# Attention scores in 32 by 32 tiles of TensorE in place of 32 by 128, on one core

## The chip, the core and the metric

The kernel runs on 1 core of a Trainium2 chip. The metric is device time in microseconds (us) for one execution. The core has five engines that run their own instruction streams and meet at semaphores: TensorE (PE in the profile, with its weight loads shown apart as PEld), ScalarE (ACT), VectorE (DVE), GpSimd (POOL) and SyncE (SP, which issues DMAs).

## The reference

The inputs are x (2048 rows of 512), wq (512x512), wk and wv (512x16), wo (512x512), w1 (512x1792) and w2 (1792x512), all bf16. There are 32 query heads of 16 dimensions and a single key/value head that all of them share.

```python
xn = layernorm(x)
q = (xn @ wq) in 32 heads of 16;  k = xn @ wk;  v = xn @ wv
p = softmax(q @ k.T * 16 ** -0.5)
s = (p @ v, heads side by side) @ wo
g = silu(silu(xn @ w1) @ w2)
out = x + s * g
```

The change touches only how the scores q @ k.T are computed.

## The kernel before

**Stages.** The 2048 queries are cut into 4 chunks of 512, the 2048 keys into 16 tiles of 128. Eight groups of four heads each make up a chunk, so there are 32 groups. A block is one head of a group, one key tile and one chunk of queries: 128 keys by 512 queries of scores, one bank of PSUM. After the scores, a block goes through an exponential, and then into the product with the values, which also sums the exponentials (half of the 32 columns of the value operand hold ones, so that the divisor comes out of the same product).

**Exponentials on two engines.** Two blocks of one key tile go to psA[0] or psA[1] (1024 columns each, used in turn), and ScalarE turns them into bf16 weights in one ACTIVATE of 128x1024 (`exp_A`, L655). Other blocks go to psD (two banks, "D" and "D1") or psF, one bank each, and VectorE turns them into a 16-bit integer whose bits are a rough bf16 exponential (`exp_D`, L693); GpSimd adds two shifted copies (`shift`, L718), and the three versions, weighted, are summed in the value product.

**TensorE's shapes.** The 128 by 128 array is used in three tilings:
- row tiles, 32 rows by 128 columns, at `tile_position=(32 * i, 0)`: the scores. The four heads of a group lie in the four row groups of qT and kT, 32 partitions each (16 used), so row tiles i of several blocks can run at the same time, each into a bank of its own. `score` (L616) makes one block's product, `burst` (L629) strings together the products of one call.
- column tiles, 128 rows by 32 columns, at `tile_position=(0, 32 * i)`: the value products (`emit_PV`, L736, recorded at L778, four heads into the four 32-partition quarters of psO), and all dense products for q, the two feed-forward layers and the output projection (`columns`, L399, recorded at L402). Some scores for VectorE are made in this shape too, from a copy of q with the other heads zeroed (`col_fill`, L1349).
- the whole array: transposes, k, v and warm-up products, mostly in the first 30 us.

The last group's first key tiles are done in two halves of 256 queries (`run_half`, L662, product at L671), in row tiles.

**The order.** The program is planned while it is built: the class `Sched` holds each engine's queue, works out the waits from what each operation reads and writes, and keeps a small model of the engines' times. The main loop at L1412 fills the time up to the next score burst with column products, then calls `score_run` (L1271), which issues two blocks for ScalarE (`fill_A`, L646) and, in the same row tiling, blocks for VectorE in the rows that are left (`fill_D`, L1365). In the plan, a burst for ScalarE may start once ScalarE has finished the exponential before last (`release`, L1205), and should start early enough for ScalarE's next (`needed`, L1208). Per ScalarE exponential there is usually one burst of three blocks and two quartets of column products.

The plan charges a row burst by the rows it names and not by the products that are issued in it, so the order of the operations comes from the call below, whatever the closures `made` contain:

```python
return op("pe", f, reads=sorted({k for _, rd in made for k in rd}, key=str), writes=writes,
          cost=("row", [blk[1] for blk, _ in items], NQ))
```

Only the last product of a burst raises the semaphore that ScalarE or VectorE waits for.

Of the kernel before, what the change touches and what calls it, by code (L numbers as in the profile page):

```python
# [13 lines left out]
P = 128  # L14
# [199 lines left out]
def bass_recurrent_scan__grouped_kv_mqa__dense_activation_silu__prompt_kernel(  # L214
# [69 lines left out]
        P=(0.25, 3.0, 0.65, 10, 1.2, 2.0, 0, 12, 0.2, 3, 3, 0.0, 0.35, 0.43, 0, 0.33, 0, 1, 9, 9),  # L284
# [12 lines left out]
        c=(0.2, 3.0, 0.7, 10, 1.6, 2.0, 0, 12, 0.2, 3, 3, 0.0, 9, 0.43, 0, 0.33, 0, 0, 0.6, 9),  # L297
# [3 lines left out]
    with ExitStack() as es:  # L301
        def sb(name, shape, dt=BF16):
            return es.enter_context(nc.sbuf_tensor(name, shape, dt))
# [12 lines left out]
        kT_sb = [sb("kTa_sb", [P, S]), sb("kTb_sb", [P, S])]  # L316
        vaug_sb = sb("vaug_sb", [P, 1 + NPH, NKT, 32])
        qT_sb = sb("qT_sb", [P, 2, NDC, NQ])
# [297 lines left out]
        def score(blk, ap):  # L616
            (gi, kt), i = blk
            c, g = gi // NG, gi % NG
            if ("q", c, g // 2) not in tok:
                raise ValueError(f"no q for {c}, {g}")  # L620
            rd = [("qT", c % 2, g // 2), "qTb", ("kT", 1, kt // 2, i) if g % 2 else ("kT", 0, kt // 2 if kt else "first")]

            def f(e):
                return e.matmul(ap, lhsT=kT_sb[g % 2][32 * i:32 * i + 32, kt * P:(kt + 1) * P],  # L624
                                rhs=qT_sb[32 * i:32 * i + 32, c % 2, g // 2, :],
                                start=True, stop=True, tile_position=(32 * i, 0))
            return f, rd

        def burst(items, writes):  # L629
# [871 lines left out]
        c = NC - 1  # L1501
# [92 lines left out]
```

## Time and profile before

| what | before |
|---|---|
| median of 2 runs | 661.67 us (661.33 to 662.02) |
| the profiled execution | 661.39 us |
| its span, first to last instruction | 659.6 us |
| TensorE products, weight loads | 8199, 8201 |
| score products in row tiles into psA (L624) | 684 + 632, 385 ns each as recorded |
| score products in row tiles into psD (L624) | 325 + 287, 385 ns |
| score products in row tiles into psF (L624) | 34 + 30, 385 ns |
| exponentials on ScalarE (L655) | 662, 630.5 us busy |
| exponentials on VectorE (L693) | 437.2 us busy in psD's two largest groups |
| granted TensorE clock, mean | 0.999 |

The time recorded for one product is longer than the time that the next one has to wait, since products are pipelined and run side by side in different tiles; the distance between starts says more. Two neighbouring exponentials on ScalarE overlap in the same way: 1221 ns is recorded for one, and they start 0.90 us apart when scores are there. A "releaser" is the event that ended an engine's idle time, and the chain of waits follows such events back from the last instruction.

### The profile page before, as it was taken

What the parts mean: (1) busy time and instruction counts of PE and PEld (TensorE: products, weight loads), DVE (VectorE), ACT (ScalarE), POOL (GpSimd) and SP (SyncE); (2) the same over time, 40 slices, a digit from 0 to 9 for tenths busy, and PEclk for the clock granted to TensorE, in tenths of its full rate; (3) what the DMA queues carried; (4) which work ended last, traced back from release to release, by engine and by line L of the source; (5) the groups of instructions that cost most, each with busy time, mean ns of one, the idle gap of its engine ahead of it and who ended that gap; (6) DMA issues with size and microseconds to landing.
All of it is one profiled execution on the core that took longest, in us unless ns stands there. A gap on an engine that the chain in (4) does not pass through costs nothing.

```text
span 659.6 us, 18816 instructions
## 1 busy us (share of the span) xinstructions
PE 649.5 (98%) x8199; PEld 185.3 (28%) x8201; DVE 596.3 (90%) x1023; ACT 652.0 (99%) x754; POOL 384.2 (58%) x388
## 2 busy tenths in 40 slices
PE   9999999999999999999999999999999999999996
PEld 4422222222222222222222222222222222222221
DVE  7999889989889989999989889999989898898995
ACT  8999999999999999999999999999999999999997
POOL 4265665557656647566665656565665565664562
PEclk9999999999999999999999999999999999999999
DMA  5450000000000000000000000010000000000110
GB/s 171 151 164 1 2 8 5 10 2 4 3 2 9 18 26 18 24 3 2 10 1 10 2 3 2 8 33 26 26 3 5 1 10 14 2 2 2 33 34 33
DMA packets 15394, 14.61 MB, mean 22 GB/s; under 512 B 3536, under 2 KB 14800, under 8 KB 15312
## 3 DMA queue, kind: packets, MB, share of 16 engines
q1 hardware_dynamic: 14752, 12.89, 6.5%
q8 instruction: 64, 1.05, 0.7%
q10 hardware_dynamic: 560, 0.52, 0.2%
q14 instruction: 18, 0.15, 0.1%
HBM read 8.95 MB, written 2.10 MB: 17 GB/s over the span
## 4 chain that ended last, share of the span: by engine, by line
ACT 83%; PE 16%; DVE 1%; issue 0%
ACT pa_sb L655 78%; PE psO L778 6%; ACT t_sb L1094 5%; PE psA L624 5%; PE psF L402 3%; PE psF L409 1%; PE psA L671 0%; DVE wq_sb L1527 0%; DVE otr_sb L888 0%; DVE xn_sb L894 0%; PE psD L624 0%; PE psD L478 0%; DVE wq_sb L1522 0%; PE psO L493 0%; DVE onb_sb L890 0%
## 5 line engine op out<-in xcount | busy, mean ns | idle before, releaser
L655 ACT ACTIVATE pa_sb<-psA 128x1024 bf16<-128x1024 f32 x662 | 630.5, 1221 | 0.6 <-PE psA L624 0.6
L718 POOL INT64_ADD ph_sb<-ph_sb x290 | 299.9, 1047 | 197.9 <-DVE ph_sb L693 197.7
L693 DVE TENSOR_SCALAR ph_sb<-psD 128x512 int16<-128x512 f32 (+1 forms) x520 | 348.0, 689 | 34.0 <-PE psD L624 29.2
L778 PE MATMUL psO<-ph_sb,vaug_sb 128*32 128x512 bf16 x1740 | 214.5, 383 | 0.0
L778 PE MATMUL psO<-pa_sb,vaug_sb 128*32 128x512 bf16 (+1 forms) x1332 | 201.3, 382 | 0.6 <-DVE onb_sb L890 0.6
L624 PE MATMUL psA<-qT_sb,kTa_sb 32*128 32x512 bf16 x684 | 132.8, 385 | 2.2 <-ACT pa_sb L655 0.9
L624 PE MATMUL psA<-qT_sb,kTb_sb 32*128 32x512 bf16 x632 | 122.5, 385 | 1.2 <-ACT pa_sb L655 0.5
L624 PE MATMUL psD<-qT_sb,kTb_sb 32*128 32x512 bf16 x325 | 114.3, 385 | 0.0
L718 POOL INT64_ADD x_sb<-x_sb x72 | 74.2, 1043 | 45.6 <-DVE x_sb L693 45.6
L624 PE MATMUL psD<-qT_sb,kTa_sb 32*128 32x512 bf16 x287 | 100.1, 385 | 0.0
L693 DVE TENSOR_SCALAR x_sb<-psD 128x512 int16<-128x512 f32 x132 | 89.2, 684 | 11.4 <-PE psD L624 9.2
L778 PE MATMUL psO<-x_sb,vaug_sb 128*32 128x512 bf16 x432 | 77.6, 383 | 0.0
L624 PEld LDWEIGHTS psA<-qT_sb,kTa_sb 32*128 32x128 bf16 x684 | 32.3, 91 | 142.7 <-ACT pa_sb L655 129.2
L402 PE MATMUL psF<-xnT_sb,w_sb 128*32 128x512 bf16 x896 | 69.8, 384 | 0.0
L402 PE MATMUL psF<-w_sb,u_sb 128*32 128x512 bf16 x896 | 69.5, 384 | 0.0
L624 PEld LDWEIGHTS psA<-qT_sb,kTb_sb 32*128 32x128 bf16 x632 | 29.8, 91 | 135.2 <-ACT pa_sb L655 122.5
L778 PEld LDWEIGHTS psO<-ph_sb,vaug_sb 128*32 128x32 bf16 x1740 | 53.3, 95 | 46.8 <-issue 29.9
L778 PEld LDWEIGHTS psO<-pa_sb,vaug_sb 128*32 128x32 bf16 x1332 | 49.0, 95 | 39.7 <-issue 29.4
L1094 ACT ACTIVATE t_sb<-psF 128x512 bf16<-128x512 f32 x72 | 57.9, 805 | 0.0
L1126 DVE SCALAR_TENSOR_TENSOR u_sb<-t_sb,psF 128x512 bf16<-128x512 bf16 x56 | 38.1, 680 | 4.7 <-ACT t_sb L1094 4.3
L693 DVE TENSOR_SCALAR ph_sb<-psF 128x512 int16<-128x512 f32 x52 | 35.4, 681 | 0.0
L624 PEld LDWEIGHTS psD<-qT_sb,kTb_sb 32*128 32x128 bf16 x325 | 27.6, 91 | 1.8 <-DVE ph_sb L693 1.3
(133 smaller groups left out, 366.7 us busy)
## 6 DMA issues: line engine op xcount, KB each, us to landing
w_sb<-in_B_w_dram SPq DMA_DIRECT2D x2, 1792.0 KB, 7.7
x_sb<-in_A_x_dram SPq DMA_DIRECT2D x18, 128.0 KB, 2.2
qm_sb<-qT_sb SPq DMA_DIRECT2D x64, 32.0 KB, 1.8
out_dram<-ob_sb SPq DMA_DIRECT2D x14, 128.0 KB, 1.7
x_sb<-in_A_x_dram SPq DMA_DIRECT2D x3, 512.0 KB, 6.4
wop_sb<-in_A_wo_dram SPq DMA_DIRECT2D x1, 512.0 KB, 4.4
wq_sb<-in_A_wq_dram SPq DMA_DIRECT2D x1, 384.0 KB, 5.8
x_sb<-in_A_x_dram ACTq DMA_DIRECT2D x2, 128.0 KB, 2.9
```

What stands on the lines that cost most here:

```text
L402: r = e.matmul(bank[32 * i:32 * i + 32, :], lhsT=lhsT[:, 32 * i:32 * i + 32], rhs=rhs, start=start, stop=stop, tile_position=(0, 32 * i), ...
L409: r = e.matmul(bank, lhsT=zero_sb[:, 0:P], rhs=zero_sb[:, :], start=True, stop=True)
L624: return e.matmul(ap, lhsT=kT_sb[g % 2][32 * i:32 * i + 32, kt * P:(kt + 1) * P], rhs=qT_sb[32 * i:32 * i + 32, c % 2, g // 2, :], start=T ...
L655: d = op("a", lambda e: e.activation(pa_sb[:, sl, :], psA[k][:, :], ACT.Exp, scale=ESCALE), reads=["A%d" % k], writes=[("pa", sl)], cost=2 ...
L693: d = op("v", lambda e: e.tensor_scalar(ph_ap(0, sl, 512 * pos, 512 * pos + m), src, float(PH_ONE + PH_BIAS), 0.0, op0=ALU.add, op1=ALU.ma ...
L718: d = op("gp", lambda e, j=j: e.int64_add(ph_ap(j, sl, 0, 4 * NQ).bitcast(I64), ph_ap(0, sl, 0, 4 * NQ).bitcast(I64), PH_SHIFT[j] * 0x0001 ...
L778: r = e.matmul(psO[32 * i:32 * i + 32, cs], lhsT=vaug_sb[:, p["v"], p["kt"], :], rhs=p["ap"], start=s0, stop=s1, tile_position=(0, 32 * i) ...
L1094: op("a", lambda e: e.activation(t_sb[:, n % 2, :], bank_ap(b), ACT.Tanh, scale=0.5 if jb[0] == "h" else 0.25), reads=[b], writes=[("t", n ...
L1126: op("v", lambda e: e.scalar_tensor_tensor(out=dst, in0=t_sb[:, n % 2, :], scalar=1.0, in1=src, op0=ALU.add, op1=ALU.mult), reads=tk["read ...
```

## The change

In `score`, the closure that issued one product of 32 rows and 128 columns issues four of 32 rows and 32 columns. Each takes 32 of the key tile's 128 keys as its weights and writes the 32 partitions of the bank that belong to those keys. The four read the same 512 queries. They stand one behind the other in the burst, at tile positions (32i, 0), (32i, 32), (32i, 64) and (32i, 96).

```diff
             def f(e):
-                return e.matmul(ap, lhsT=kT_sb[g % 2][32 * i:32 * i + 32, kt * P:(kt + 1) * P],
-                                rhs=qT_sb[32 * i:32 * i + 32, c % 2, g // 2, :],
-                                start=True, stop=True, tile_position=(32 * i, 0))
+                for j in range(4):
+                    r = e.matmul(ap[32 * j:32 * j + 32, :], lhsT=kT_sb[g % 2][32 * i:32 * i + 32, kt * P + 32 * j:kt * P + 32 * j + 32],
+                                 rhs=qT_sb[32 * i:32 * i + 32, c % 2, g // 2, :],
+                                 start=True, stop=True, tile_position=(32 * i, 32 * j), skip_group_check=True)
+                return r
             return f, rd
```

Everything else stays as it is: `run_half` keeps its row tiles, the column products keep theirs, and the queues of all engines hold the same operations in the same order, with 7968 products in place of 1992 in the changed lines.

## The prediction

> **What bounds the kernel now.** I read the page first (busy shares, then the chain that ended last), then the timeline of TensorE, of its weight loads and of ScalarE around 300 us, then the start times of the single records, then the waits.
>
> ```profile
> PE 649.5 (98%) x8199; PEld 185.3 (28%) x8201; DVE 596.3 (90%) x1023; ACT 652.0 (99%) x754; POOL 384.2 (58%) x388
> ...
> ACT 83%; PE 16%; DVE 1%; issue 0%
> ```
>
> Two engines are full. The chain runs through ScalarE for 83%, nearly all of it the exponentials of L655, and through TensorE for most of the rest. So ScalarE leads, and TensorE steps in wherever it is late.
>
> ```profile
> 300.32 0.39 PE L624 MATMUL psA<-qT_sb,kTa_sb 32*128 32x512 bf16 x2
> 300.33 0.39 PE L624 MATMUL psD<-qT_sb,kTa_sb 32*128 32x512 bf16 x1
> 300.64 0.62 PE L402 MATMUL psF<-xnT_sb,w_sb 128*32 128x512 bf16 x8
> 301.19 0.39 PE L624 MATMUL psA<-qT_sb,kTa_sb 32*128 32x512 bf16 x2
> 301.20 0.39 PE L624 MATMUL psD<-qT_sb,kTa_sb 32*128 32x512 bf16 x1
> 301.51 0.83 PE L778 MATMUL psO<-ph_sb,vaug_sb 128*32 128x512 bf16 x12
> ```
>
> Here the reader sees one beat: a score burst in row tiles (two products for ScalarE, one for VectorE), a change of tiling, products in column tiles, a change back. From 300.32 to 301.19 is 0.87 us. The records to the nanosecond: the burst's three products start at 300.321, .325 and .328; the first column product at 300.642; its three companions 3 to 4 ns apart; the second four 0.217 us after the last of the first four; the next burst 0.311 us after the last column product. A stream of 512 columns takes 0.213 us (products of 512 columns step by 0.216 us, those of 256, L493, by 0.109, so 256 columns are 0.107), which leaves about 0.10 us for each change of tiling. Counted so over the trace, it is 0.102 us from row to column tiles (633 times) and 0.098 us back (634 times, medians).
>
> ScalarE's exponentials start 0.903 us apart when nothing holds them; with the 72 tanh (0.476 us each) the floor of its stretch is 662 x 0.903 + 72 x 0.4765 = 632 us, and the starts exceed the floor by 9.3 us in sum, at 197 places where the scores came late. TensorE waits in its turn. Counting starts beyond the usual change or step, I find 9.7 us in 205 changes into a score burst, 9.4 us in 103 places within a burst (VectorE's bank not yet free), and 3 us elsewhere: about 22 us. TensorE needs 660 - 22 = 637 us, ScalarE 660 - 9 = 650 us; their mutual waits make the rest.
>
> ```profile
> PEld psA L624 <- ACT pa_sb L655: 251.7, 584, 0.8
> ```
>
> This wait looks like much free time and is not. 251.7 us over 584 is 0.43 us each, and in the timeline above 0.42 us of such a gap is the column products still streaming (0.3 us after the last load) and the 0.1 us change. What is truly free is the 9.7 us above.
>
> **The change, part by part.** It replaces each of 684 + 632 products into psA and 325 + 287 + 34 + 30 into psD and psF, 1992 in all, by four: 5976 more products and as many more loads. The changed program has 7968 of them in the same places and order; no engine's sequence or wait is otherwise different. The half bursts at the end (L671) and the masked scores in column tiles stay.
>
> *The extra tiles.* A burst of three blocks becomes twelve tiles of the array, all different, so their streams can overlap and only their starts are staggered. The nearest row for that is the first quartet after a change into column tiles, where four loads and four products alternate: 3.34 ns per product (mean of 636). Two products in row tiles are 3.4 ns apart (1258 times). I take 3.35 ns: nine more tiles make the usual burst 30 ns longer, and 5976 x 3.35 ns = 20.0 us in all. This lies on TensorE's own path.
>
> The Trainium skill, "TensorE: Matmul & The Clock Gate", section "Measured speedup vs the span model", gives about 4 ns per tile, also for sixteen tiles of 32 by 32. By it the sum would be 23.9 us (an estimate from that page).
>
> *The bounds of one more tile.* Below: nothing, if starts in different row and column groups coincide; no row shows two starts at once, so no gain. Above: the products of L519 (128x16), each with a load of the whole array, start 25 ns apart, which would make 5976 x 25 = 149 us. Loads of 32 columns are nearer to the column quartet (95 ns each there against 91 ns in row tiles, and hidden in both), so I keep 3.35.
>
> *The supply of instructions.* A beat now needs 20 pairs of load and product in 0.9 us, 45 ns a pair, against 11. The densest long stretch is 40 products in 2.2 us, 55 ns each, so the rate is not shown outright. But at 169.75 us TensorE's queue stops in a semaphore instruction for 51 ns; the first load follows at 169.826, and four pairs have all started by 169.867, 65 ns after the stop: 16 ns a pair. Queued instructions need not be that fast, and the drain of 0.1 us before each burst covers the rest: nothing. Fetching them adds 11952 to 18816 instructions; the page has 64 instruction packets at 0.7% of 16 engines' span, 1.2 us each. Some 41 more cost nothing while the DMA engines stand at 0 tenths, and 47 us if each were waited for.
>
> *What is late next.* The scores for ScalarE come 20 ns later in a burst (six more starts) and those for VectorE 30 ns later. Half of the exponentials have less than 0.08 us to spare, so this reaches ScalarE in most beats once TensorE has no rest left. VectorE at 90% has 63 us of gaps and mostly runs behind its banks (it waited for psD only 143 times, 38.5 us), so it takes the delay without becoming the bound.
>
> *The sum.* A beat with two quartets needs 0.869 us of TensorE and now 0.899, against 0.903 of ScalarE: just enough. Beats with three quartets already exceed it and are paid for by rests elsewhere. Of the 20.0 us, what TensorE now waits at changes into a burst, 9.7 us, is taken up, because those rests exist only where it was early; the 9.4 us within bursts are banks that VectorE frees, which I leave as they are. Net +10.3 us. On the profiled execution (661.4 us, its span of 659.6 us and 1.8 us around it; the median of the two runs shown is 661.67): 671.7, say 672 us. Ends of this term: all 22 us of rest taken up, -2 us, which ScalarE's floor turns into about 0 (661); none taken up, +20 us (681).
>
> **Rivals.**
>
> *A: the changes of tiling become cheaper,* since column products and the new scores share 32-column tiles. There are 633 + 634 changes; 16 ns less on each pays for the 20 us, and at half price (0.05 us, 63 us saved) ScalarE alone would bound: 661.4 - 9.3 = 652 us. Against it: counted in the same way, changes of rows or of columns alone are no cheaper (whole array to row tiles 0.098 us, to column tiles 0.094, row tiles to whole array 0.104). That is -1.4%, not a clear gain. Chance 7%.
>
> *B: the change doesn't cost what it says, the delay vanishes in TensorE's rests* or the starts coincide: 659 to 664 us. For it: TensorE's 637 + 20 = 657 us is still less than the span. Against: the rests lie in short pieces next to a full ScalarE. Chance 8%.
>
> *C: more per tile or more waiting,* 5 to 10 ns a pair because loads no longer hide in a burst of twelve, or some instruction packets waited for: 5976 x 7 = 42 us, less 10 of rest, 693 us; 680 to 715 for the span of these. It decides from 4.5 ns per pair upward. Chance 12%.
>
> *D: the four loads of one row of tiles wait for that row's running products.* Then the four streams of a row follow one another: 3 x 0.217 us more in 650 bursts, 423 us, about 1085 us. The column quartets speak against it: there all four tiles share the same 128 rows, and the second load starts 4 ns after the first product. A milder form is 31 ns for each exposed load (the delay from a load at 33.285 us to its product at 33.317): 185 us, about 845. Chance 4%.
>
> The rule behind D is in the Trainium skill, "TensorE: Matmul & The Clock Gate", section "The mechanism": a load overlaps running products only when its row group differs. By that rule D would happen; the trace differs at the column quartets, and no run here shows row and column groups combined.
>
> **How the numbers follow.** The forecast case has 69%, from about 665 to 681 us, likeliest 672. About 2% is what a measurement of this kernel tells from no change: 648.4 and 674.9 us. A third of the forecast case lies above 674.9 (rests less usable than I take), 22%; with C and D slower comes to 38%. Same: 47% of the forecast, A and B, 61%, less 1% for a faster case, as ScalarE's work leaves at most 652 us unless its beat itself shortened. The range leaves out A, part of B, and the upper half of C with D: 663 to 690 us.
>
> **What would show it.** In the profile after: single products of a burst 3 to 4 ns apart, bursts ending 30 ns later (right), or 7 ns and more, or starts 0.217 us apart within a row (C, D). Changes of tiling still 0.10 us; about 0.05 is A. The chain's TensorE share should rise well above 16%, ScalarE should start to show idle time before L655, and rests before bursts should shrink from 9.7 us towards 0. If ScalarE still leads with 83%, B was right. The forecast is wrong if a burst's stagger is other than 3.35 ns per tile, or if VectorE's banks turn out to be the next wait.

## The result and the profile after

The changed kernel takes 668.57 us (median of 2 runs, 668.28 to 668.85) against 661.67 us: 6.9 us more, a ratio of 1.0104 with a 95% interval of 1.0061 to 1.0148. The profiled execution took 668.85 us with a span of 667.0 us, 7.4 us longer than the span before. The forecast was 672 us, in a range of 663 to 690, with a difference within 2% as the likeliest outcome. The times and ratios below are of runs with a granted clock of 0.986 or more; one run of the second experiment with tiny products, at 0.978 and 714.65 us, is left out of them.

The page after, its lines of engines and of the chain that ended last (share of the span, by engine):

```profile
PE 658.5 (99%) x14175; PEld 202.3 (30%) x14177; DVE 599.0 (90%) x1023; ACT 657.4 (99%) x754; POOL 384.2 (58%) x388
...
PE 75%; ACT 21%; DVE 2%; DMA 0%; issue 0%; SPq 0%
```

The busy shares hardly tell that anything happened: both engines were full and still are. The chain does. Before, 83% of it was ScalarE's; now 75% is TensorE's. ScalarE's row shows little more idle time (0.6 us before, 2.6 us now), but the time recorded for one exponential fell from 1221 to 1056 ns: a start that comes late stands less long behind the exponential before it.

```profile
L655 ACT ACTIVATE pa_sb<-psA 128x1024 bf16<-128x1024 f32 x662 | 630.5, 1221 | 0.6 <-PE psA L624 0.6
L657 ACT ACTIVATE pa_sb<-psA 128x1024 bf16<-128x1024 f32 x662 | 623.7, 1056 | 2.6 <-PE psD L625 1.2
```

(The first line is from the page before, the second from the page after.)

The timeline of TensorE (start us, recorded us, line, what, how many) shows one beat of the changed kernel:

```profile
300.37 0.39 PE L402 MATMUL psF<-xnT_sb,wq_sb 128*32 128x512 bf16 x4
300.69 0.41 PE L625 MATMUL psA<-qT_sb,kTa_sb 32*32 32x512 bf16 x8
300.72 0.40 PE L625 MATMUL psD<-qT_sb,kTa_sb 32*32 32x512 bf16 x4
301.04 0.62 PE L402 MATMUL psF<-xnT_sb,wq_sb 128*32 128x512 bf16 x8
301.59 0.41 PE L625 MATMUL psA<-qT_sb,kTa_sb 32*32 32x512 bf16 x8
301.62 0.40 PE L625 MATMUL psD<-qT_sb,kTa_sb 32*32 32x512 bf16 x4
```

The twelve products run side by side: those into psA take 0.41 us together in place of 0.39, and the blocks for VectorE start 0.03 us after those for ScalarE. By the single records, the twelve starts lie between 300.692 and 300.728, 3.3 ns apart, and the column products follow 0.314 us after the last one, as before. The beat is 0.90 us long, it was 0.87.

The waits of TensorE's loads ahead of a burst for ScalarE (us in total, times, longest) stand in three rows, which go by what is taken to have ended the wait: an exponential, a tanh, or nothing that the profile shows. Before, the rows beside the line shown in the prediction were

```profile
PEld psA L624 <- ACT t_sb L1094: 16.5, 39, 0.4
PEld psA L624 <- issue: 7.9, 22, 0.5
```

and now the three are

```profile
PEld psA L625 <- ACT pa_sb L657: 224.9, 537, 0.7
PEld psA L625 <- ACT t_sb L1096: 25.0, 59, 0.4
PEld psA L625 <- issue: 15.4, 43, 0.4
```

47 waits fewer are put down to an exponential, and 41 more to the other two: most of them only changed rows. In sum it is 276.1 us in 645 waits before and 265.3 us in 639 after, 10.8 us less. What is left, 0.42 us each, is little but the column products still streaming and the change of tiling.

**TensorE's ledger.** What a start-to-start count of the records gives, in three sums: starts within score bursts (from the first product of a burst to its last), changes from a burst to column products, and changes back (both beyond the 0.213 us of the last stream, so rests are in them).

| us | within bursts | changes to columns | changes to rows | sum | span |
|---|---|---|---|---|---|
| before | 20.2 | 65.4 | 72.0 | 157.6 | 659.6 |
| after | 38.1 | 65.5 | 61.8 | 165.4 | 667.0 |
| after less before | +17.9 | +0.1 | -10.2 | +7.8 | +7.4 |

The sums account for the whole difference. 17.9 us is the stagger of the new products (19.6 us) less 1.7 us of waits within bursts that have gone (9.4 us before, 7.7 after; 1.0 of the 7.7 is a single stop at 49.5 us, taken up below). Of the 10.2 us, about 9 are rests before bursts (9.7 us in 205 places before, about 1 us after). The rest is the change itself, which is 3 ns shorter into the new tiles (median 0.096 us against 0.099).

### The profile page after: what moved, and what is told of

The parts are those of the page before. It is cut to its first block, busy times and chain, and to the rows that moved or that the text cites. A ratio compares the mean times of both kernels' runs of the same rounds, so it can differ in the third digit from the quotient of the medians.

```text
span 667.0 us, 30768 instructions
## 1 busy us (share of the span) xinstructions
PE 658.5 (99%) x14175; PEld 202.3 (30%) x14177; DVE 599.0 (90%) x1023; ACT 657.4 (99%) x754; POOL 384.2 (58%) x388
## 4 chain that ended last, share of the span: by engine, by line
PE 75%; ACT 21%; DVE 2%; DMA 0%; issue 0%; SPq 0%
PE psO L780 27%; PE psA L625 26%; ACT pa_sb L657 20%; PE psF L402 18%; PE psD L625 2%; PE psD L402 2%; ACT t_sb L1096 1%; DVE stats_sb L418 1%; DMA x_sb<-in_A_x_dram 0%; DVE ph_sb L695 0%; DVE xn_sb L451 0%; PE psF L625 0%; PE psA L673 0%; PE psD L462 0%; PE psD L493 0%
## 5 line engine op out<-in xcount | busy, mean ns | idle before, releaser
L657 ACT ACTIVATE pa_sb<-psA 128x1024 bf16<-128x1024 f32 x662 | 623.7, 1056 | 2.6 <-PE psD L625 1.2
L625 PE MATMUL psA<-qT_sb,kTa_sb 32*32 32x512 bf16 x2736 | 139.3, 385 | 0.9 <-DVE kTa_sb L505 0.4
L625 PE MATMUL psA<-qT_sb,kTb_sb 32*32 32x512 bf16 x2528 | 128.1, 385 | 0.3 <-ACT pa_sb L657 0.3
L625 PE MATMUL psD<-qT_sb,kTb_sb 32*32 32x512 bf16 x1300 | 117.4, 384 | 0.0
L625 PE MATMUL psD<-qT_sb,kTa_sb 32*32 32x512 bf16 x1148 | 102.8, 385 | 0.8 <-issue 0.6
L625 PEld LDWEIGHTS psA<-qT_sb,kTa_sb 32*32 32x32 bf16 x2736 | 38.0, 88 | 137.8 <-ACT pa_sb L657 115.5
L625 PEld LDWEIGHTS psA<-qT_sb,kTb_sb 32*32 32x32 bf16 x2528 | 35.1, 88 | 129.8 <-ACT pa_sb L657 109.4
L1096 ACT ACTIVATE t_sb<-psF 128x512 bf16<-128x512 f32 x72 | 46.0, 639 | 0.0
L625 PEld LDWEIGHTS psD<-qT_sb,kTb_sb 32*32 32x32 bf16 x1300 | 30.1, 88 | 1.9 <-DVE ph_sb L695 1.3
```

Source lines behind the costliest of these rows:

```text
L625: r = e.matmul(ap[32 * j:32 * j + 32, :], lhsT=kT_sb[g % 2][32 * i:32 * i + 32, kt * P + 32 * j:kt * P + 32 * j + 32], rhs=qT_sb[32 * i:32 ...
L657: d = op("a", lambda e: e.activation(pa_sb[:, sl, :], psA[k][:, :], ACT.Exp, scale=ESCALE), reads=["A%d" % k], writes=[("pa", sl)], cost=2 ...
L1096: op("a", lambda e: e.activation(t_sb[:, n % 2, :], bank_ap(b), ACT.Tanh, scale=0.5 if jb[0] == "h" else 0.25), reads=[b], writes=[("t", n ...
```

## The experiments

The open questions: is it TensorE's time that makes the difference, with the rests taken up first (theory 1)? Or does a constant share of every added ns reach the end (theory 2)? Or does the loss come from scores that reach ScalarE later? The records show more lateness than the stagger explains: from the last score product's start to the start of its exponential it is 425 ns before and 456 ns after wherever the scores were what the start waited for.

**Two products per block in place of four: 32 by 64.** The edit is shown against the changed kernel, with the middle of its lines left out (`...`).

```diff
-                for j in range(4):
-                    r = e.matmul(ap[32 * j:32 * j + 32, :], lhsT=kT_sb[...][..., kt * P + 32 * j:kt * P + 32 * j + 32],
+                for j in range(2):
+                    r = e.matmul(ap[64 * j:64 * j + 64, :], lhsT=kT_sb[...][..., kt * P + 64 * j:kt * P + 64 * j + 64],
```

> Each score product becomes two of 32 rows by 64 columns: 1992 more products in place of 5976, so at 3.35 ns each TensorE gets 6.7 us more. Theory 1 (TensorE's stagger is paid for first out of its rests, 9.7 us before bursts; what is left goes to the end): nearly all taken up, +0 to +2.5 us, rests before bursts down from 9.7 to about 4 us. Theory 2 (a constant share of each added ns reaches the end, 6.9 of 20.0 us, since beats are each full or not): +2.3 us, with ScalarE's lateness up in proportion. For the delay from ScalarE's last score product to its exponential (425 ns before, 456 after): if it grows with the number of products per exponential (2, then 8) it is about 435 here with 4; if it belongs to 32-column tiles it is 425; if to any splitting of the columns, 456.

Measured: 664.0 us against 661.62 (ratio 1.0036, interval 1.0024 to 1.0048), +2.4 us. That is in the range of both theories, so the time alone decides nothing. The ledger does:

| us, less before | within bursts | changes to columns | changes to rows | sum | span |
|---|---|---|---|---|---|
| 32 by 64 | +4.3 | +8.3 | -9.9 | +2.7 | +2.6 |

The stagger was smaller than for 32 by 32, as expected, but a change from tiles of 64 columns back to column products takes 0.115 us in place of 0.102, 633 times. So 12.6 us were added, not 6.7, and 9.9 us came back at the changes to rows: rests before bursts fell to 1.3 us, and this change too is 3 ns shorter. The expectation missed the slower change to columns, and it had the rests fall only to about 4 us. A constant third of 12.6 us would have been 4.3 us, not 2.4.

**The four products in reverse order,** columns 96, 64, 32, 0 (`for j in (3, 2, 1, 0)`).

> The four products of a block in the order of columns 96, 64, 32, 0. Stagger and changes as in the changed kernel, so +6.9 us by either theory of the time. It asks about the delay of 456 ns from the last product's start to the exponential: if the 31 ns more belong to the column group of the last product (96), the delay falls to 425 to 440 and ScalarE's scores are earlier by that much, which would show what this lateness is worth: at most 3 us back if it matters. If they belong to the number of products or to 32-column tiles as such, 456 ns and no change in time.

Measured: 668.26 us (1.0099, 1.0086 to 1.0112), the time of the changed kernel, and 456 ns from the last product to the exponential. The column group of the last product has no part in either.

**More stagger, without other work.** Each burst starts with products of one query in some of its tiles; their results are overwritten.

```diff
             def f(e):
                 for m, _ in made:
+                    m(e, True)
+                for m, _ in made:
                     r = m(e)
...
-                for j in range(4):
+                for j in (3,) if pre else range(4):
+                    n = 1 if pre else NQ
```

> As the changed kernel, and each score burst begins with one extra product of a single query (one column) per block, in the last column group, later overwritten: 1992 more products, 6.7 us more of stagger at 3.35 ns. Theory 1: the rests before bursts are used up after the change (0.9 us left), so nearly all of it reaches the end: +6.9 + 6 = about +13 us. Theory 2 (a constant third): +9.2 us. If a tile that is used twice in a burst waits 25 ns, as the narrow whole-array products do, the last product of the first block shows it.

> As the changed kernel, with one extra single-query product ahead of each of its products: 7968 more, 26.7 us more of stagger at 3.35 ns. Theory 1: rests are gone (0.9 us before bursts, 7.7 within them), so +6.9 + 24 to 27 = +31 to +34 us. Theory 2: +6.9 + 9 = +16 us. If each first real product has to wait 25 ns for its tile's tiny one, another 12 ns per block come on top, 24 us.

(The second run has `range(4)` for `(3,)`.) Measured: 679.5 us (1.027, 1.0256 to 1.0283), +17.9 us, and 704.27 us (1.0656, 1.0628 to 1.0683), about +43 us. Both are more than either theory said (13 and 9 us; 31 to 34 and 16 us), because of what the expectations named as a possibility: a tile used twice in a burst waits. The timeline of the run with one tiny product each:

```profile
300.61 0.37 PE L626 MATMUL psA<-qT_sb,kTb_sb 32*32 32x512 bf16 x1
...
300.62 0.39 PE L626 MATMUL psF<-qT_sb,kTa_sb 32*32 32x1 bf16 x4
300.64 0.37 PE L626 MATMUL psD<-qT_sb,kTb_sb 32*32 32x512 bf16 x1
300.66 0.37 PE L626 MATMUL psF<-qT_sb,kTa_sb 32*32 32x512 bf16 x1
300.96 0.39 PE L783 MATMUL psO<-ph_sb,vaug_sb 128*32 128x512 bf16 x2
```

The last real product of a block, in the tile that its tiny one had used, starts 38 to 39 ns after the tiny one (300.624 to 300.663 by the records), so a usual burst became 35 ns longer, not 10. Part of this comes back: after such a last product the change to columns takes 0.088 us in place of 0.102, and ScalarE starts 444 ns after it in place of 456. The ledger takes both in:

| us, less before | within bursts | changes to columns | changes to rows | sum | span |
|---|---|---|---|---|---|
| one tiny product | +36.6 | -8.7 | -10.7 | +17.2 | +18.0 |
| four tiny products | +60.6 | -8.7 | -10.6 | +41.3 | +41.7 |

Between 12.6 us added (32 by 64) and 51.9 us (60.6 - 8.7), the changes to rows give back 9.9 to 10.7 us, always the same rests and the 3 ns per change, and everything beyond that reaches the end. Theory 2 falls: with the share that the changed kernel lost (10.2 of 18.0 us added came back), 29 of the 51.9 us would have come back, not 10.6.

**TensorE given rests in other places.** To see whether the change costs anything where TensorE has time, two omissions, each in the kernel before and in the changed one. First, the middle products of both feed-forward layers run over 256 columns:

```diff
                 for m in items:
                     l, r = pair(m)
-                    h = columns(e, ap, l, r, m == 0, m == end)
+                    n = 256 if k in ("h", "z") and 0 < m < end else NQ
+                    h = columns(e, ap[:, 0:n], l, r[:, 0:n], m == 0, m == end)
```

> The kernel before, where the middle products of both feed-forward layers run over 256 columns in place of 512 (the other half of these sums is left out): 56 x 2 + 16 x 12 = 304 quartets shorter by 0.107 us, 32.5 us less work for TensorE, nothing else changed. Control for the next run. TensorE's rests grow from 22 to some 50 us, and ScalarE's floor takes over: at most the 9.3 us of ScalarE's lateness can go, so 653 to 660 us.

> The same omission in the changed kernel. Theory 1 (the change costs TensorE's time alone, and 20 us of stagger go into rests where there are any): the difference to the run before it shrinks from 6.9 us to 0 to 2.5 us; it is not zero, because the rests come with the feed-forward products and a beat without them has none. Rival (what costs is that scores come 51 ns later to ScalarE, 20 ns of stagger and 31 ns of delay): this stays in every beat, so the difference stays at 5 to 7 us.

Measured: 661.69 us for the kernel before (1.0006, 0.9996 to 1.0015) and 663.62 us for the changed one (1.0036, 1.0024 to 1.0049). The difference fell from 6.9 to 1.9 us, as theory 1 has it. The control itself missed: with 32 us less for TensorE the kernel before did not get faster at all. Why is shown under "What bounds it" below.

Second, the value products too, so that TensorE rests in most beats:

```diff
-                        r = e.matmul(psO[32 * i:32 * i + 32, cs], lhsT=vaug_sb[:, p["v"], p["kt"], :], rhs=p["ap"],
+                        lt = not s0 and not s1 and cs.stop - cs.start == NQ
+                        r = e.matmul(psO[32 * i:32 * i + 32, slice(0, 256) if lt else cs], lhsT=vaug_sb[:, p["v"], p["kt"], :],
+                                     rhs=p["ap"][:, 0:256] if lt else p["ap"],
```

> The kernel before, with the omission of the light pair and with all value products but a group's first and last over 256 of 512 queries (half of these sums is left out): about 800 more quartets shorter by 0.107 us, some 118 us less for TensorE in all, now in every beat. The light kernel stayed at 661.7 us although TensorE had 32 us less to do, so ScalarE's lateness sits in beats that the feed-forward products do not touch. If long runs of value products make ScalarE late there, that lateness (about 10 us) goes: 651 to 656 us. If VectorE or the plan's fixed order holds it, 659 to 662 us.

> The same omission in the changed kernel. Theory 1 (the change costs TensorE's time alone): with rests in every beat the 30 ns of a burst vanish in them, and the difference to the run before it, 1.9 us in the light pair, falls to between -0.5 and +1 us. Rival (part of the loss is that scores are 51 ns later for ScalarE in every beat): 1.9 us or more stays.

Measured: 663.47 us (1.0026, 1.0016 to 1.0037; the nine runs lie between 661.82 and 665.08) and 662.10 us (1.0011, 1.0002 to 1.0020). The change costs nothing here. By the medians it is even 1.4 us less, below the range of theory 1, but the runs spread by more than that and the fastest are alike (661.82 and 661.85). The pages of the two, engines and chain, first the kernel before and then the changed one:

```profile
PE 562.4 (85%) x8201; PEld 186.7 (28%) x8201; DVE 597.1 (90%) x1023; ACT 652.2 (99%) x754; POOL 384.3 (58%) x388
...
ACT 97%; DMA 1%; DVE 1%; SPq 0%; PE 0%; issue 0%
```

```profile
PE 582.0 (88%) x14177; PEld 206.8 (31%) x14177; DVE 597.4 (90%) x1023; ACT 652.4 (99%) x754; POOL 384.2 (58%) x388
...
ACT 95%; PE 2%; DVE 2%; issue 0%
```

TensorE's busy time differs by 19.6 us, about the stagger, and the time does not follow: ScalarE is the chain in both. The later scores are there as well (425 and 456 ns), so this lateness is worth nothing as long as TensorE can start a burst early enough. That rival has fallen for the kernel with rests; in the changed kernel itself the ledger leaves it no room, since TensorE's three sums already make 7.8 us where the span grew by 7.4.

**Only the blocks for VectorE split.** (The edit against the changed kernel, in part.)

```diff
-        def score(blk, ap):
+        def score(blk, ap, split=True):
...
+                if not split:
+                    return e.matmul(ap, lhsT=kT_sb[g % 2][32 * i:32 * i + 32, kt * P:(kt + 1) * P], ...
...
-            made = [score(blk, ap) for blk, ap in items]
+            made = [score(blk, ap, writes[0][0] != "A") for blk, ap in items]
```

> Only the blocks for VectorE are split in four; those for ScalarE stay in tiles of 32 by 128. Within a burst TensorE then goes from 32x128 to 32x32 tiles in other row groups. If any change of tiling drains the array: in some 560 bursts with such blocks, the second kind starts 0.31 us after the first in place of 4 ns, about 175 us more for TensorE, less rests of 10 to 20: 810 to 830 us. If tilings with the same row groups run side by side: 650 x 3 x 3.35 ns = 6.5 us of stagger, at most +2 us. The delay from the last product to VectorE's start (458 ns before, 503 after, where VectorE waited): 503 if it belongs to 32x32 tiles, about 470 if it grows with the number of products side by side.

Measured: 823.46 us, in a single run and so without an interval. The timeline of TensorE:

```profile
300.73 0.39 PE L625 MATMUL psA<-qT_sb,kTb_sb 32*128 32x512 bf16 x2
301.05 0.39 PE L629 MATMUL psD<-qT_sb,kTb_sb 32*32 32x512 bf16 x4
301.38 0.40 PE L402 MATMUL psF<-w_sb,u_sb 128*32 128x512 bf16 x4
```

The two kinds of tiles lie in different rows of the array and still follow each other at 0.32 us (569 times, median 0.315): a whole stream of 0.213 us and 0.10 us of change. So tiles of two shapes did not run side by side here, although they differ in columns alone and share no rows, and the change cost what the others cost. The delay to VectorE was 437 ns, neither of the two values expected; it is taken up below.

**The plan told of the extra products.**

```diff
-                      cost=("row", [blk[1] for blk, _ in items], NQ))
+                      cost=("row", [(blk[1], j) for blk, _ in items for j in range(4)], NQ))
```

> The changed kernel, with a plan that charges a burst for each of its products (4 ns per further tile), so that the order of all work is made anew. Theory 1: TensorE's sum of work is the same and it stays the bound, so the time stays within -2 to +4 us of the changed kernel; a new order can lose a little because the plan's settings were chosen for the old charge. If the 6.9 us came from an order that no longer fits the durations, most of it comes back: 662 to 664 us.

Measured: 686.14 us (1.0371, 1.0357 to 1.0385). Neither expectation held, and the question stays unanswered, since the new plan moved work between engines. Its group of exponentials on ScalarE (busy us, mean ns of one):

```profile
L657 ACT ACTIVATE pa_sb<-psA 128x1024 bf16<-128x1024 f32 x683 | 650.1, 1207 | 3.9 <-PE psD L625 2.7 <-PE psA L625 1.2
```

683 in place of 662: 21 more at the 0.917 us that ScalarE needs for one (see the next section) are 19.3 us, about what this run lost against the changed kernel (17.6 us). Counted as in the next section, its ends come late in 13 steps, by 4.3 us in sum.

## Why the prediction was right

**What bounds it.** "TensorE needs 637 us, ScalarE 650, their mutual waits make the rest" was right in that the two were close and TensorE had about 22 us of rest. The other half was wrong: ScalarE had no rest at all in the kernel before. The prediction counted ScalarE's starts. They can be 0.903 us apart, and the 9.3 us by which they exceeded that in sum were taken for scores that came late. But a start can run ahead and then stand behind the exponential before it. The recorded ends tell what ScalarE gets done: in the kernel before they are 0.917 us apart for an exponential and 0.490 us for a tanh, and of 733 such steps only one is more than 6 ns longer (by 11 ns). The chain of before, where it stays on ScalarE, shows the same beat (start us, us, what, how many):

```profile
424.45 16.50 ACT pa_sb L655 x18
464.91 17.41 ACT pa_sb L655 x19
515.95 11.92 ACT pa_sb L655 x13
```

16.50 us for 18, 17.41 for 19 and 11.92 for 13 are 0.917 us each. The kernel's own plan charges the same (`model`, L122: 0.0635 us + 1024 / 1200). So the floor of ScalarE's stretch is 662 x 0.917 + 72 x 0.490 = 642 us and not 632, and the stretch of before is at this floor: 11 us to the end of its first exponential, 641 to the end of its last, 7 after it, 659.6 in all. That is why 32 us and then 118 us less work for TensorE moved nothing.

With the floor right, the loss can be counted on ScalarE too. The steps between ends that are more than 6 ns too long, in the profiled execution of each run:

| run | late steps of 733 | their excess, us | span less before, us |
|---|---|---|---|
| before | 1 | 0.0 | |
| after | 82 | 7.4 | +7.4 |
| 32 by 64 | 45 | 2.5 | +2.6 |
| reverse order | 83 | 6.4 | +6.7 |
| one, four tiny products | 162, 487 | 17.6, 41.3 | +18.0, +41.7 |
| only VectorE's blocks split | 537 | 161.8 | +162.1 |
| first omission, before and changed | 8, 25 | 2.1, 1.7 | +2.1, +1.9 |
| both omissions, before and changed | 2, 4 | 0.3, 0.5 | +0.4, +0.7 |

In every row the late steps make the whole difference, within 0.4 us. In the changed kernel 80 of the 82 belong to exponentials that start 456 ns after their last score product, as those do that waited for their scores: TensorE's bursts came too late in some 80 places, and in the other 650 steps ScalarE is as fast as ever. That 75% of the chain is now TensorE's does not mean that ScalarE rests: the chain follows starts, and a start that waited for its scores counts for TensorE even where no end came later for it. (The first omission in the kernel before was profiled in one of its longer runs, 663.56 us; two of its eight late steps, 1.0 and 0.6 us, make most of the 2.1 us.)

That ScalarE's beat is 0.917 us also says what the rests were: times in which TensorE was early. The wrong floor did not enter the forecast's sum, which went by TensorE's rests, so it cost the forecast nothing; that was luck. With the right floor rival A's 652 us was out of reach, and the usual beat of 0.899 us had 18 ns to spare against ScalarE's, not 4.

**The extra tiles: 20.0 us.** Measured 19.6 us: 17.9 us more within bursts, and 1.7 us of waits gone from there. The column quartet was the right row to take the price from, for twelve tiles as for four. The span model of the Trainium skill ("TensorE: Matmul & The Clock Gate", section "Measured speedup vs the span model"), 4 ns per tile, would have given 23.9 us by estimate; these records have 3.3 ns.

**Supply of instructions, loads, fetches at nothing.** Right but for one place: twelve products start in 36 ns from one queue, and 47 more instruction packets (111 against 64, some 41 expected) go unnoticed, except that at 49.5 us TensorE stops for 1.0 us between two products of one block, where the profile shows nothing that it waits for:

```profile
PEld psD L625 <- issue: 0.9, 1, 0.9
```

ScalarE's end at 53.5 us comes 1.05 us late for it, the longest of the 82 late steps counted above. The run with the products in reverse order has as many products and no such stop, and its span is 0.7 us shorter. Whether an instruction packet was waited for is not shown. Rivals C and D are out. With D goes the rule of the Trainium skill, "TensorE: Matmul & The Clock Gate", section "The mechanism", that a load overlaps running products only in other row groups: within a burst four tiles share their rows, and their loads start 3.4 ns apart.

**Rests taken up: 9.7 us.** Measured about 9 us (9.7 before, about 1 left), 1.3 us left with 32 by 64 and 0.6 us left in both runs with tiny products. This step, the one that was chosen between -22 and 0, carried the forecast. Two smaller terms were set at nothing and were not: 1.7 us of the waits within bursts went too, and the change into the new tiles is 3 ns shorter, which makes 1 to 2 us over 634 changes. Those are the 3 us between +10.3 and +6.9.

**What is late next.** The scores were said to come 20 and 30 ns later. They came 51 and 75 ns later (20 + 31 for ScalarE; 30 + 45 for VectorE), see below. The pair with both omissions shows that this cost nothing where TensorE had rests. "This reaches ScalarE in most beats" was wrong: an end came late in 82 steps of 733.

**Rivals.** A, cheaper changes of tiling, is out except for the 3 ns: between tiles of 32 columns but different rows the change still costs 0.096 to 0.102 us. B, absorption, is what happened to half of the cost, and all of it when TensorE had rests everywhere.

## What to carry to other kernels

A tiling with more and smaller tiles is not free where TensorE is close to its limit: each further product delayed the array's next change by 3.3 ns, which the busy shares of the full kernel hardly show (98 and 99%), since streams overlap. Before pricing a small addition to an engine's path, count its rests start by start, at the places where the addition falls; they are taken up first, and beyond them the price is paid in full. Of two full engines the one that sets the time is found by taking work from the other: here 118 us less of TensorE's work moved nothing. And where the instructions of an engine overlap, measure its beat from end to end: starts can run ahead, and what they then lose looks like waiting.

## What was not expected of the hardware

**Completion comes later with more products side by side.** From the start of a burst's last product to the start of the engine that reads it, where that start waited for the scores (medians, ns):

| burst | ScalarE | VectorE |
|---|---|---|
| before: 2 products, then 1 | 425 | 458 |
| 32 by 64: 4, then 2 | 450 | 486 |
| after: 8, then 4 | 456 | 503 |
| only VectorE's split: 2 alone, 4 alone | 425 | 437 |

From before to after it is 31 ns for 6 more products and 45 ns for 9 more, 5 ns each; the products of 64 columns are recorded 13 ns longer by themselves (398 against 385 ns). VectorE's four alone come sooner than its one product behind two others, although they are more. The Trainium skill, "TensorE: Matmul & The Clock Gate", section "The cost: per-tile semaphore tail", gives 4.7 ns per tile and 26.3 ns per semaphore increment. Estimates by these figures agree with the trace: 6 x 4.7 = 28 and 9 x 4.7 = 42 ns against 31 and 45, and for the last row one tile more and one increment less, 4.7 - 26.3 = -22 ns against 437 - 458 = -21. No run here varied the increments alone.

**Tiles of 64 columns leave slower:** 0.115 us to column tiles, against 0.102 from tiles of 128 or of 32 columns.

**A tile used twice in a burst** waits 38 ns from the start of a one-column product to the next product's start. Some 13 ns of them are not lost: what follows such a product comes 12 to 14 ns sooner after it (0.088 against 0.102 us; 444 against 456 ns).

**ScalarE's starts and ends keep different beats:** exponentials of 1024 columns can start 0.903 us apart for a while and end 0.917 us apart.
